# Query and key rows kept in DRAM as three slots of one stride, in a fused attention and feed-forward block

## The chip, the cores and the metric

The kernel runs on one core of a Trainium2 chip. Its time is device microseconds for one execution. The core has five engines that run side by side, each through its own list of instructions in order: TensorE (PE, matrix products), VectorE (DVE), ScalarE (ACT), GpSimd (POOL) and SyncE (SP, which here only issues transfers). Transfers (DMAs) are issued by SP and by ACT, and move data between DRAM and the on-chip memory (SBUF, 128 partitions) while the engines compute. Products land in PSUM banks, from which DVE and ACT copy them out.

## The reference

One transformer block over S = 2048 tokens of D = 640 features, all in f32: sliding-window attention with 32 heads of 20 features and a window of 256 keys, then a gated feed-forward layer of F = 1536.

```python
def _A_ref(x, wqkv, wo):                       # H = 32, Dh = 20, W = 256
    qkv = (x @ wqkv).reshape(B, S, 3, H, Dh).transpose(2, 0, 3, 1, 4)
    q, k, v = qkv[0], qkv[1], qkv[2]
    scores = jnp.einsum("bhqd,bhkd->bhqk", q, k) * (Dh ** -0.5)
    mask = (idx[:, None] - idx[None, :] >= 0) & (idx[:, None] - idx[None, :] < W)
    p = softmax(jnp.where(mask, scores, -1e9))
    o = jnp.einsum("bhqk,bhkd->bhqd", p, v)
    return o.transpose(0, 2, 1, 3).reshape(B, S, D) @ wo

h = x + _A_ref(layernorm(x), A_wqkv, A_wo)
h2 = h + (gelu(layernorm(h) @ w_gate) * (layernorm(h) @ w_up)) @ w_down
```

## The kernel before

**Numbers in two parts.** To keep f32 accuracy on f16 products, an operand is split into a high f16 part (`hi`) and a low one (`lo`, the rest), and a product of two operands is the sum of three: high with high, high with low, low with high.

**Tiling.** Tokens go in 16 blocks of 128 (`B[j]`) and 8 chunks of two blocks (`C[c]`, 256 tokens, `CW`). For each chunk, `qk(c, 0)` computes the queries and `qk(c, 1)` the keys, as features by tokens: five tiles of 128 features (`KC = 5`), two to a PSUM bank of the name `mm`, so three banks' worth (two tiles, two tiles, one tile). There are two such banks. The very first, `qk(0, 0)`, uses f32 products on the raw weights; the other 15 use three f16 products. `vproj(j)` computes the values of a block in two halves, in the same two banks.

**From product to stacked rows.** `qk_out` (line 750) empties a bank: ACT writes the high part into a tile `qks`, DVE writes the low part beside it, and the bank is free (`done("mm")`). Then ACT issues one transfer (line 764) that stores the tile to a DRAM buffer `qk<c><which>` of 640 feature rows, each with its high and its low 256 tokens. `qks` is a ring of two tiles, and line 754 lets ACT begin a tile only when fewer than two are begun and not yet stored. After the third store `stack(c, which, d)` (line 771) starts: from DRAM it loads, for each of the two heads of a pair (`par`), three sets of 20 rows into partitions 64 x par + 0..59 of `qT` (queries, one tile a chunk) or `kT` (keys, a ring of six blocks): high, high, low for queries and high, low, high for keys. One product over 60 rows then gives the three-part sum. So a chunk has 12 such loads, each of 20 partitions with 16 runs of 256 tokens (512 bytes), 160 KB, issued by SP. The host orders the features of the weights (line 1684) as (head of the pair, feature of the head, pair), so the first half of the 640 rows belongs to `par = 0`.

**Around it.** For each block, `maxima` (line 842) forms raw scores with 60-row products and DVE takes each row's largest after adding a mask (`max_out`, line 914; `mask` for the first two blocks, `band` after); the maxima go back as two more rows of `qT` (partitions 60, 61, against rows of `kT` that hold powers of two, set by `big_lane`), and `scores` (line 959) forms the scores again with 62-row products, already less the maximum. ACT takes the exponential into `pt`, POOL sets masked entries to zero, `value_lane` multiplies by the values, `normalise` divides (it copies `pv` through the tile `oT`), and `wo_block` projects. The feed-forward layer follows (the last scores are formed at 566 us) and shares no code with the change.

**What sets the order.** All instructions are put out by a program that runs ahead of time: a loop (line 1632) over lanes (generators) with a model of the chip, `Clock`. Each step names its engine and when its inputs will be ready by the model; `cost` (line 214) gives durations, `box` (line 74) says which bytes an access touches, `issue` (line 162) advances the model's time, with at most eight transfers in flight (`window`, line 69). The order on each engine comes out of this model; on the chip each engine runs through its list and waits where data is late. While no score has been formed and TensorE would be idle in the model, the loop puts out a product of `ident16` with itself into `pv` (line 1663), a placeholder without use for the result. `stack` waits in the model for the stores, for `pos["big"]`, and for the weights (chunks 0 and 1) or for block 2c-3 having been scored; for chunks from 2 on its loads are spread out by `PACE`.

Of the kernel before, what the change touches and what calls it, by code (L numbers as in the profile page):

```python
# [11 lines left out]
F32 = mybir.dt.float32  # L12
F16 = mybir.dt.float16
BF16 = mybir.dt.bfloat16
# [8 lines left out]
P = 128  # L23
# [30 lines left out]
class Clock:  # L54
# [18 lines left out]
    @staticmethod  # L73
    def box(ap):

        t = ap.tensor
        size = mybir.dt.size(ap.dtype)
        (ps, pn), *free = [tuple(x) for x in ap.ap]
        if ap.space == DRAM:
            n = 1 + sum((c - 1) * abs(st) for st, c in [(ps, pn), *free])  # L80
            return t.name, (0, 1, ap.offset * size, (ap.offset + n) * size, n * size, 1, 1)
        if ps:
            p0, f0 = divmod(ap.offset, ps)
        else:
            p0, f0 = 0, ap.offset
        n = 1 + sum((c - 1) * abs(st) for st, c in free)
        step, count = max(((abs(st), c) for st, c in free if c > 1), default=(n, 1))
        run = n - (count - 1) * step
        if run >= step:
            run, count = n, 1  # L90
        return t.name, (p0, p0 + pn, f0 * size, (f0 + n) * size, run * size, step * size, count)
# [98 lines left out]
class Engine:  # L190
# [23 lines left out]
    def cost(self, op, out, ins):  # L214
        n = out.free_size()
        if op.startswith("dma_start"):
            size = math.prod(c for _, c in out.ap) * mybir.dt.size(out.dtype)
            if op == "dma_start_transpose":
                return size / 150e3
            wide = mybir.dt.size(out.dtype) == 4 or out.space == DRAM  # L220
            return size / (380e3 if wide else 150e3)
        half = mybir.dt.size(out.dtype) == 2 and ins and mybir.dt.size(ins[0].dtype) == 2
        if self.name == "tensor":
            n = ins[1].free_size()
            if op == "transpose":
                n = ins[0].partition_size()
            passes = 1 if mybir.dt.size(ins[0].dtype) == 2 else 2 if op == "transpose" else 4
            rows, cols = ins[0].partition_size(), out.partition_size()
            mode = "full" if op == "transpose" else "row" if rows <= 64 else "col"
            mode = "full" if mode == "col" and cols > 32 else mode  # L230
            k = self.clock
            switch, k.mode = SWITCH * (k.mode != mode), mode
            at = out.start_partition() + (ins[0].start_partition() // 4 if mode == "row" else 0)
            beside, k.half = mode != "full" and at > k.half and not switch, at
            if beside:
                return 0.0005
            return switch + k.warmth(max(n * passes / 2400, 0.027), rows) + 0.0027
        if self.name == "vector":
            m = max([n] + [i.free_size() for i in ins])
            if op == "tensor_copy" and half or op == "tensor_scalar" and m > 320:  # L240
                return (0.065 if half else 0.185) + 0.00053 * m
            return 0.065 + 0.00106 * m + 0.06 * (op == "scalar_tensor_tensor" and len(ins) == 3)
        if self.name == "scalar":
            return 0.00084 * n + (0.05 if op == "copy" or len(ins) == 1 else
                                  0.14 if ins[0].space == PSUM else 0.18)
        if self.name == "gpsimd":
            if op == "memset":
                return 0.06 + 0.0008 * n
            return 0.46 if n == 1 else 0.06 + (0.00105 if op == "affine_select" else 0.00203) * n
        raise NotImplementedError(self.name)  # L250
# [3 lines left out]
def block_kernel(ctx: ExitStack, tc: tile.TileContext, x, wqkv, wo, wg, wu, wd, out):  # L254
# [67 lines left out]
    def on(eng, *reads, when=None, after=None):  # L322
        f = need(*reads, when=when, eng=eng)
        if after is not None:
            return (eng,), lambda: max(f(), nc.others(after, eng))
        return (eng,), f
# [14 lines left out]
    nc.vector.tensor_copy(ident16, ident)  # L341
    mhalf = const.tile([P, 1], F32, name="mhalf")
    nc.vector.memset(mhalf, -0.5)
    ones = const.tile([P, P], F32, name="ones")
    nc.vector.memset(ones, 1.0)


    NS = 16
# [229 lines left out]
    def ff_scales_down(fg):  # L578
# [19 lines left out]
    gu = gu.rearrange("p (a c f) -> p a c f", c=KC, f=512)  # L598

    HB = P // 2  # L600
    mask = wp.tile([P, 2 * P], F32, name="mask")
    nc.gpsimd.memset(mask, 0.0)
    nc.gpsimd.affine_select(mask[:, P:2 * P], mask[:, P:2 * P], pattern=[[-1, P]],
                            compare_op=ALU.is_ge, fill=NEG, base=0, channel_multiplier=1)
    band = wp.tile([P, 5 * HB], F32, name="band")
    nc.gpsimd.memset(band, 0.0)
    for a in range(2):
        first, last = band[HB * a:HB * a + HB, 0:HB], band[HB * a:HB * a + HB, 4 * HB:]
# [116 lines left out]
    def qk(c, which):  # L725
# [3 lines left out]
        if not first:  # L729
            xh, xl = C[c].x  # L730
            wh, wl = w.hl
        d = dram.tile([D, 2, CW], F16, name=f"qk{c}{which}")
        left = [3]
        for t0 in range(0, KC, 2):
            ts = range(t0, min(t0 + 2, KC))
# [14 lines left out]
    def qk_out(c, which, ts, ps, d, left):  # L750

        o = ps[:, :len(ts) * CW].rearrange("p (t n) -> p t n", n=CW)
        up = qs if c == which == 0 else _pow2(QE)
        yield on("scalar", ps, when=lambda: pos["qk"] < pos["qks"] + 2 and (c or pos["qs"]))
        pos["qk"] += 1
        st = nc.tile(wq, [P, 2, 2, CW], F16, "qks", 2)
        hi, lo = (st[:, :len(ts), i, :] for i in range(2))
        nc.scalar.activation(hi, o, AF.Copy, scale=up)
        yield on("vector", hi, after=ps)
        nc.vector.scalar_tensor_tensor(lo, o, up, hi, op0=ALU.mult, op1=ALU.subtract)  # L760
        done("mm")
        both = st[:, :len(ts)].rearrange("p t m n -> p t (m n)")
        yield on("scalar", both)
        nc.scalar.dma_start(d[ts[0] * P:(ts[-1] + 1) * P].rearrange("(t p) m n -> p t (m n)", p=P),
                            both)
        pos["qks"] += 1
        left[0] -= 1
        if not left[0]:
            side.append((LATE, stack(c, which, d)))

    def stack(c, which, d):
        yield ("sync",), need(d, when=lambda: pos["big"] == 2 and (W["q"].ready if c < 2 else
                                                                B[2 * c - 3].scored), eng="sync")
        if which == 0:
            C[c].qT = at("qT", [P, H // 2, CW], F16)
            for b in (2 * c, 2 * c + 1):
# [3 lines left out]
            s = 2 * c % RK  # L780
            to = kT[:, :, s:s + 2, :].rearrange("p i r n -> p i (r n)")
        for par in range(2):
            for m, i in enumerate(((0, 0, 1), (0, 1, 0))[which]):
                rows = slice(64 * par + DH * m, 64 * par + DH * m + DH)
                if c > 1:
                    yield ("sync",), lambda: nc.moved["sync"] - PACE
                nc.sync.dma_start(to[rows], d.rearrange("(a d i) m n -> a m d i n", a=2,
                                                        d=DH)[par, i])
        C[c].stacked += 1
        if C[c].stacked == 2:  # L790
            for b in (2 * c, 2 * c + 1):
# [886 lines left out]
def _layout(inputs):  # L1678
# [2 lines left out]
    f = lambda n: np.asarray(inputs[n])  # L1681
    c = np.ascontiguousarray
    wqkv = f("A_wqkv").reshape(KC, P, 3, D).transpose(2, 1, 0, 3).copy()
    order = np.arange(D).reshape(H // 2, 2, DH).transpose(1, 2, 0).reshape(-1)
    wqkv[:2] = wqkv[:2][..., order]
    rows = lambda a: a.reshape(KC, P, FG, F // FG).transpose(2, 1, 0, 3)
    return {
# [29 lines left out]
```

## Time and profile before

| | |
|---|---|
| median of three runs | 1014.78 us (1012.98 to 1014.88) |
| the profiled execution | 1015.33 us |
| its span, first to last instruction | 1013.6 us |
| busy PE / DVE / ACT / POOL | 996.3 / 754.7 / 442.5 / 315.0 us |
| mean granted TensorE clock | 0.997 of full |
| loads of query and key rows on SP's queue | 48 and 48, 160 KB each |
| stores of query and key tiles on ACT's queue | 32 of 256 KB and 16 of 128 KB |

A row of the grouped view reads: line, engine, operation, output <- inputs, shape, xcount | busy us, mean ns of one | idle time of the engine just before them and what ended it. Every instruction goes through one helper, so all have line L199, and one goes by names of tiles. A row of the order of time reads: start us, duration us, engine, line, operation, names, shape, count [idle before <- what ended it]. SPq and ACTq are the transfer issues of SP and ACT. A row of the windows gives the stretch, its length, busy time of PE, PEld (weight loads), DVE, ACT and POOL, the granted clock, the share of the DMA engines and GB/s. Matmul records overlap, since products are pipelined.

### The profile page before, as it was taken

How to read it: one execution, taken by the hardware profiler on the slowest of the kernel's cores; microseconds unless marked ns; L12 is line 12 of the kernel's file. 1: busy time of each engine (PE TensorE's matmuls, PEld its weight loads, DVE VectorE, ACT ScalarE, POOL GpSimd, SP SyncE). 2: the span in 40 equal slices, each digit the busy share in tenths (PEclk: the TensorE clock that was granted, in tenths of full speed). 3: DMA queues.
4: the chain of work that ended last, by engine and by line, in shares of the span. 5: the costliest groups of instructions: out<-in, count | busy, mean ns of one | idle time of the engine just before them, and what ended most of it. 6: DMA issues, size and time to landing. Idle time of an engine off the chain costs nothing.

```text
span 1013.6 us, 30516 instructions
## 1 busy us (share of the span) xinstructions
PE 996.3 (98%) x12798; PEld 696.4 (69%) x12798; DVE 754.7 (74%) x2212; ACT 442.5 (44%) x711; POOL 315.0 (31%) x504
## 2 busy tenths in 40 slices
PE   8999999999999999999999999999999999999998
PEld 7876777666666776776655654577777777777776
DVE  7888999786667877676688687798888875544553
ACT  5516666654555555554567634432222212221220
POOL 7004344643344333332345311254313300000000
PEclk9999999999999999999999999999999999999999
DMA  8658775291271714236004342323453542222211
GB/s 308 148 127 177 185 163 167 67 166 41 71 133 39 143 55 88 64 79 188 18 29 133 68 130 92 98 107 116 144 187 102 148 142 78 79 103 80 78 53 52
DMA packets 105834, 112.67 MB, mean 111 GB/s; under 512 B 38368, under 2 KB 79584, under 8 KB 105696
## 3 DMA queue, kind: packets, MB, share of 16 engines
q1 hardware_dynamic: 93600, 99.97, 36.7%
q10 hardware_dynamic: 12096, 10.75, 3.5%
q8 instruction: 100, 1.64, 0.7%
q14 instruction: 38, 0.31, 0.1%
HBM read 73.73 MB, written 28.84 MB: 101 GB/s over the span
## 4 chain that ended last, share of the span: by engine, by line
PE 86%; DVE 7%; DMA 3%; ACT 2%; issue 1%; SPq 1%; POOL 0%; ACTq 0%; DVEq 0%
PE mm L199 44%; PE pv L199 12%; PE ra L199 12%; PE rb L199 10%; PE tp L199 7%; DVE junk L199 1%; DMA kT<-qk 1%; SPq L199 1%; DVE am L199 1%; DMA wst<-in_wu_dram 1%; DMA qT<-in_wqkv_dram 1%; DMA wst<-in_wg_dram 1%; ACT pt L199 1%; DVE ht L199 0%; DVE w1l L199 0%
## 5 line engine op out<-in xcount | busy, mean ns | idle before, releaser
L199 POOL TENSOR_SCALAR_AFFINE_SELECT pt<-pt 128x512 f32<-128x512 f32 x352 | 174.8, 512 | 297.0 <-ACT pt L199 281.3
L199 DVE CUSTOM_DVE_ANT_0 junk<-rb,band 128x320 bf16<-128x320 f32 x228 | 111.5, 489 | 53.4 <-PE rb L199 48.8
L199 ACT ACTIVATE pt<-ra,esc 128x640 f32<-128x640 f32 (+2 forms) x132 | 100.6, 770 | 74.3 <-PE ra L199 69.3
L199 DVE CUSTOM_DVE_ANT_0 junk<-ra,band 128x320 bf16<-128x320 f32 x220 | 107.7, 489 | 33.2 <-PE ra L199 26.8
L199 ACT ACTIVATE pt<-rb,esc 128x640 f32<-128x640 f32 (+2 forms) x124 | 94.1, 764 | 82.4 <-PE rb L199 73.2
L199 PE MATMUL pv<-pt,v 128*21 128x128 f32 x2880 | 104.7, 279 | 0.0
L199 PEld LDWEIGHTS <-ah 128*128 128x128 f16 x768 | 75.1, 98 | 29.2 <-issue 1.9
L199 ACT ACTIVATE gel<-gel,ffk 128x512 f32<-128x512 f32 x36 | 26.0, 722 | 134.3 <-DVE gel L199 134.3
L199 PEld LDWEIGHTS pv<-pt,v 128*21 128x21 f32 x2880 | 70.0, 101 | 9.9 <-issue 1.0
L199 PEld LDWEIGHTS <-ws 128*128 128x128 f16 x720 | 70.5, 98 | 8.1
L199 PEld LDWEIGHTS <-qT 60*64 60x64 f16 x1280 | 29.8, 104 | 61.0 <-issue 51.9
L199 PEld LDWEIGHTS <-kT 62*64 62x64 f16 x2880 | 63.4, 107 | 11.2 <-issue 7.5
L199 PEld LDWEIGHTS <-gu 128*128 128x128 f16 x440 | 41.9, 98 | 36.1 <-issue 2.5
L199 DVE SCALAR_TENSOR_TENSOR ht<-mm,ffk,ht 128x320 f32<-128x320 f32 x96 | 52.1, 545 | 13.7 <-PE mm L199 11.8
L199 ACT CAST ah<-gel 128x512 f16<-128x512 f32 x48 | 29.6, 617 | 68.7 <-DVE gel L199 68.6
L199 PE MATMUL mm<-xh,w1h 128*128 128x256 f16 x200 | 54.6, 273 | 0.8 <-DVE qks L199 0.8
L199 PE MATMUL mm<-xl,w1h 128*128 128x256 f16 x200 | 54.7, 274 | 0.0
L199 PE MATMUL mm<-xh,w1l 128*128 128x256 f16 x200 | 54.6, 273 | 0.0
L199 POOL TENSOR_TENSOR gelt<-gelt 128x256 f32<-128x256 f32 x18 | 15.3, 852 | 112.0 <-ACT gelt L199 111.9
L199 PE MATMUL mm<-w3h,oh 128*128 128x320 f16 x160 | 48.3, 302 | 1.4 <-DVE qks L199 1.4
L199 PE MATMUL mm<-w3l,oh 128*128 128x320 f16 x160 | 48.2, 301 | 0.0
L199 PE MATMUL mm<-w3h,ol 128*128 128x320 f16 x160 | 48.1, 300 | 0.0
(313 smaller groups left out, 2562.6 us busy)
## 6 DMA issues: line engine op xcount, KB each, us to landing
ws<-wsums SPq DMA_DIRECT2D x24, 640.0 KB
qk<-qks ACTq DMA_DIRECT2D x32, 256.0 KB
qT<-qk SPq DMA_DIRECT2D x48, 160.0 KB
kT<-qk SPq DMA_DIRECT2D x48, 160.0 KB
wsums<-ws SPq DMA_DIRECT2D x12, 640.0 KB
ht<-in_x_dram SPq DMA_DIRECT2D x16, 320.0 KB
h_dram<-ht SPq DMA_DIRECT2D x16, 320.0 KB
ht<-h_dram SPq DMA_DIRECT2D x16, 320.0 KB
```

Of the source, the lines that this page charges most:

```text
L199: r = real(*args, **kw)
```

## The change

The DRAM buffer becomes three slots of 640 rows, `[3, D, CW]` instead of `[D, 2, CW]`: queries as high, high, low, keys as high, low, high. ACT writes the high part twice into a `qks` tile of three parts (one instruction over an input repeated by a stride of zero), DVE writes the low part as before. Each tile of 128 features is stored by a transfer of its own, five for a query or key half instead of three, of 192 KB each. The host's feature order becomes (feature of the head, head of the pair, pair), so the three slots and the 20 features of a head lie at one stride, and `stack` reads the 60 rows of a head of the pairs by one transfer: two loads for a query or key half instead of six, 480 KB each. In DRAM such a row is 16 runs of 512 bytes in one piece.

Beside this, the third key tile of chunk 0 uses the tile `oT`, not in use yet, in place of the `qks` ring (`spare`), and does not wait for the ring. The first query loads no longer wait for the whole split query weight but for the parts that lie in the tile they overwrite, and the first key loads do not wait for it at all. `mask` and `band` become bf16, the unused `ones` goes. In the model, DRAM accesses get boxes with strides, and the rate of 2-byte loads goes from 150e3 to 170e3 bytes per us.

```diff
@@ Clock.box
         if ap.space == DRAM:
-            n = 1 + sum((c - 1) * abs(st) for st, c in [(ps, pn), *free])
-            return t.name, (0, 1, ap.offset * size, (ap.offset + n) * size, n * size, 1, 1)
-        if ps:
+            p0, pn, f0, free = 0, 1, ap.offset, [(ps, pn), *free]
+        elif ps:
@@ Engine.cost
-            return size / (380e3 if wide else 150e3)
+            return size / (380e3 if wide else 170e3)
@@ constants
-    ones = const.tile([P, P], F32, name="ones")
-    nc.vector.memset(ones, 1.0)
-    mask = wp.tile([P, 2 * P], F32, name="mask")
+    mask = wp.tile([P, 2 * P], BF16, name="mask")
-    band = wp.tile([P, 5 * HB], F32, name="band")
+    band = wp.tile([P, 5 * HB], BF16, name="band")
@@ qk
-        d = dram.tile([D, 2, CW], F16, name=f"qk{c}{which}")
+        d = dram.tile([3, D, CW], F16, name=f"qk{c}{which}")
@@ qk_out
-        yield on("scalar", ps, when=lambda: pos["qk"] < pos["qks"] + 2 and (c or pos["qs"]))
+        spare = c == 0 and which == 1 and len(ts) == 1
+        yield on("scalar", ps, when=lambda: (spare or pos["qk"] < pos["qks"] + 2)
+                 and (c or pos["qs"]))
         pos["qk"] += 1
-        st = nc.tile(wq, [P, 2, 2, CW], F16, "qks", 2)
-        hi, lo = (st[:, :len(ts), i, :] for i in range(2))
-        nc.scalar.activation(hi, o, AF.Copy, scale=up)
+        if spare:
+            st = at("oT", [P, 4, P], F32, 1).bitcast(F16).rearrange("p a n -> p (a n)")
+            st = st[:, :3 * CW].rearrange("p (t m n) -> p t m n", t=1, n=CW)
+        else:
+            st = nc.tile(wq, [P, 2, 3, CW], F16, "qks", 2)
+        twice, lo = ((st[:, :len(ts), 0:2, :], st[:, :len(ts), 2, :]),
+                     (st[:, :len(ts), 0:3:2, :], st[:, :len(ts), 1, :]))[which]
+        hi = twice[:, :, 0]
+        nc.scalar.activation(twice, o.unsqueeze(2).to_broadcast([P, len(ts), 2, CW]), AF.Copy,
+                             scale=up)
...
-        both = st[:, :len(ts)].rearrange("p t m n -> p t (m n)")
-        yield on("scalar", both)
-        nc.scalar.dma_start(d[ts[0] * P:(ts[-1] + 1) * P].rearrange("(t p) m n -> p t (m n)", p=P),
-                            both)
+        for i, t in enumerate(ts):
+            yield on("scalar", st[:, i])
+            nc.scalar.dma_start(d[:, t * P:(t + 1) * P].rearrange("m p n -> p m n"), st[:, i])
@@ stack
-        yield ("sync",), need(d, when=lambda: pos["big"] == 2 and (W["q"].ready if c < 2 else
-                                                                B[2 * c - 3].scored), eng="sync")
+        def free():
+            if c > 1:
+                return B[2 * c - 3].scored
+            return pos["big"] == 2 and (which or len(W["q"].have) > (2, KC - 1)[c])
+
+        yield ("sync",), need(d, when=free, eng="sync")
...
         for par in range(2):
-            for m, i in enumerate(((0, 0, 1), (0, 1, 0))[which]):
-                rows = slice(64 * par + DH * m, 64 * par + DH * m + DH)
-                if c > 1:
-                    yield ("sync",), lambda: nc.moved["sync"] - PACE
-                nc.sync.dma_start(to[rows], d.rearrange("(a d i) m n -> a m d i n", a=2,
-                                                        d=DH)[par, i])
+            if c > 1:
+                yield ("sync",), lambda: nc.moved["sync"] - PACE
+            nc.sync.dma_start(to[64 * par:64 * par + 3 * DH],
+                              d.rearrange("m (d a i) n -> a (m d) i n", a=2, d=DH)[par])
@@ _layout
-    order = np.arange(D).reshape(H // 2, 2, DH).transpose(1, 2, 0).reshape(-1)
+    order = np.arange(D).reshape(H // 2, 2, DH).transpose(2, 1, 0).reshape(-1)
```

## The prediction

> **What bounds the kernel now.** I read the page first (span, busy times, chain that ended last), then TensorE's waits, then the order of time around each gap.
>
> ```profile
> span 1013.6 us, 30516 instructions
> ...
> PE 996.3 (98%) x12798; PEld 696.4 (69%) x12798; DVE 754.7 (74%) x2212; ACT 442.5 (44%) x711; POOL 315.0 (31%) x504
> ...
> PE 86%; DVE 7%; DMA 3%; ACT 2%; issue 1%; SPq 1%; POOL 0%; ACTq 0%; DVEq 0%
> ```
>
> TensorE is busy in 996.3 of 1013.6 us and carries 86% of the chain. The change takes no matrix product away, so it can only win what is not product: idle time (17.3 us), placeholder products, and time at a lower clock. The placeholders are the loop's `ident16` products, issued while no score exists:
>
> ```profile
> L199 PE MATMUL pv<-ident 128*128 128x128 f16 x221 | 16.5, 239 | 2.5 <-DVE pv L199 2.5
> ```
>
> Those before 26 us cover the loading of inputs, which the change leaves alone. The later runs, in TensorE's order of time (start, duration):
>
> ```profile
> 37.95 3.29 PE L199 MATMUL pv<-ident 128*128 128x128 f16 x56
> ...
> 41.08 0.76 PE L199 MATMUL mm<-gu 128*128 128x320 f32 x2
> ...
> 51.81 0.31 PE L199 MATMUL ra<-kT,qT 60*64 60x128 f16 x8
> ...
> 70.22 1.95 PE L199 MATMUL pv<-ident 128*128 128x128 f16 x32
> ```
>
> The first run is a hole of 41.08 - 37.95 = 3.1 us, 56 ns a placeholder. Two thirds of the rest up to the first score stand in the run at 70.22 (32 of 55 or so, together some 3.1 us). The row at 51.81 is the first product that reads stacked rows (the first maxima). Of the idle time, three waits touch what is changed. First the list of waits (us in total, times, longest), then the two rows of TensorE's order that waited for key rows:
>
> ```profile
> PE mm L199 <- DVE qks L199: 2.2, 3, 0.8
> ```
>
> ```profile
> 229.55 0.32 PE L199 MATMUL rb<-kT,qT 60*64 60x64 f16 x3 [2.14 <-DMA kT<-qk]
> ...
> 297.31 0.33 PE L199 MATMUL ra<-kT,qT 60*64 60x320 f16 x3 [1.37 <-DMA kT<-qk]
> ```
>
> The two waits for key rows are 3.5 us. They cost more than that, as the windows behind them show (each row ends with granted clock, DMA share and GB/s):
>
> ```profile
> 228.00:234.00 6.00, 4.45 (x59) 2.67 (x60) 2.04 (x9) 0.79 (x1) 0.00 (x0) 0.72 0.05 10
> 297.00:301.00 4.00, 3.69 (x79) 2.71 (x78) 1.00 (x4) 0.79 (x1) 1.42 (x3) 0.57 0.80 226
> ```
>
> The clock falls to 0.57 for 4 us after the second wait, 4 x 0.43 = 1.7 us lost; around the first, 6 x 0.28 = 1.7, of which I count 1.5, since TensorE idles in a part of it. So late key rows cost 3.5 + 3.2 = 6.7 us.
>
> **Why those rows come late.** The SP queue around both places, then the chain's pieces at the second, and one store of the ACT queue:
>
> ```profile
> 200.49 3.17 SPq L199 DMA_DIRECT2D qT<-qk  x4
> ...
> 221.29 1.38 SPq L199 DMA_DIRECT2D ht<-in_x_dram  x1
> 222.72 2.36 SPq L199 DMA_DIRECT2D kT<-qk  x3
> ...
> 272.21 4.72 SPq L199 DMA_DIRECT2D qT<-qk  x6
> ...
> 283.31 9.72 SPq L199 DMA_DIRECT2D kT<-qk  x5
> ```
>
> ```profile
> 286.98 3.72 DMA qk<-qks
> ...
> 290.71 0.74 SPq L199
> ...
> 292.29 4.99 DMA kT<-qk
> ```
>
> ```profile
> 221.78 0.34 ACTq L199 DMA_DIRECT2D qk<-qks  x1
> ```
>
> Counting the 48 stores in order (three per query or key half of a chunk), the one at 221.78 is the last of chunk 4's keys. Its rows were stored 60 us before the loads that begin at 283.31; yet the load at 290.71 waited for the store of 286.98, which belongs to chunk 5. That is no data dependence. The planner's `window` (line 69, eight transfers) models it: a transfer waits for an older one to finish. Chunk 3's keys likewise sat behind an input tile's load at 221.29. From its first issue to its last byte chunk 3 took 200.49 to 229.4 (just before the product that waited; 28.9 us) and chunk 4 272.21 to 292.29 + 4.99 = 297.28 (25.1 us), where chunk 6, undisturbed, ran through:
>
> ```profile
> 393.02 4.73 SPq L199 DMA_DIRECT2D qT<-qk  x6
> 397.79 6.99 SPq L199 DMA_DIRECT2D kT<-qk  x6
> ```
>
> ```profile
> 396.00:410.00 14.00, 14.00 (x278) 9.33 (x276) 9.33 (x37) 8.77 (x14) 5.54 (x12) 1.00 0.78 126
> ```
>
> Twelve loads of 160 KB at 126 GB/s (last figure) are 15.6 us, so the last lands some 17 us after the first issue.
>
> **The change part by part.**
>
> A. *The third key tile of chunk 0 no longer waits for the ring of two `qks` tiles* (`spare`, taken from the unused `oT`). Before, ACT and DVE copied it out at:
>
> ```profile
> 36.36 0.38 ACT L199 ACTIVATE qks<-mm 128x256 f16<-128x256 f32 x1 [2.04 <-DVE sw L199]
> ...
> 39.54 0.42 DVE L199 SCALAR_TENSOR_TENSOR qks<-mm,qks 128x256 f16<-128x256 f32 x1
> ```
>
> ACT idled 2.04 us before it, DVE had other work first, and the second half of the value projection needs that bank: hence the 3.1 us of placeholders. Copied out at once (0.38 and 0.42 us, a little more for the wider write) the bank is free before 37.95. I take **-3.1 us**; bounds 0 (DVE, busy there, puts it off again) and -6.2 (the other 55 placeholders go too).
>
> B. *Six loads of 20 rows become two of 60 rows.* SP issues 32 instead of 96; each waits for its turn in the eight and can be stood behind. TensorE wanted chunk 3's keys at 229.55 - 2.14 = 227.4, 26.9 us after the first issue, and chunk 4's at 297.31 - 1.37 = 295.9, 23.7 us after. Four issues that run through like chunk 6's twelve land after 17 us at the old rate: 7 to 10 us early. The rate itself is a cost the trace doesn't show. Bounds: unchanged (126 GB/s), since key rows still land in runs of 512 bytes; or the fastest window of wide rows here, since query rows are now 8 KB whole on both sides:
>
> ```profile
> 297.00:298.00 1.00, 0.69 (x22) 0.53 (x25) 0.32 (x1) 0.10 (x1) 0.00 (x0) 0.79 1.15 350
> ```
>
> At 350 GB/s a chunk's 1.97 MB would take 5.6 us, with the 2 us of lag seen above 7.6. I take the first end, 17 us, by which B already holds. Against it: rows now alternate between the halves within each feature tile, so both loads need all five stores, where the first three of six used to need only the first four tiles. Chunks 3 and 4 had their stores long before; chunks 0 to 2 feel it, where TensorE waits for no key row now. I take **-5.0 us**, three quarters of 6.7, since a new order can place a late load elsewhere; bounds -6.7 and +2 (nothing won, and one more wait like the first at chunks 0 to 2).
>
> The Trainium skill (DMA: Bandwidth & Descriptors, Why a DMA increments its semaphore by 16, "How many engines") says a transfer spreads over the largest number up to 16 that divides both patterns' slowest dimension: 10 engines for 20 rows, 15 for 60. By it a key load of 480 KB would take two thirds of its old time and B would stay the same, only safer; no row here shows the engines one by one.
> The skill (TensorE: Matmul & The Clock Gate, Part 1) halves the clock after a whole idle window of about 3.4 us. By that neither wait would cost clock and B would shrink to three quarters of 3.5, -2.6; the 0.57 row above says that a wait of 1.4 us did cost it, and the trace decides.
>
> C. *Stores and copies grow.* Rows before:
>
> ```profile
> L199 ACT ACTIVATE qks<-mm 128x512 f16<-128x512 f32 x30 | 17.9, 596 | 16.5 <-PE mm L199 12.8 <-DMA qT<-qk 2.0 <-PE rb L199 1.4
> ...
> L199 ACT ACTIVATE qks<-mm 128x256 f16<-128x256 f32 x15 | 5.8, 383 | 8.5 <-PE mm L199 3.9 <-DVE sw L199 2.0 <-DMA qk<-qks 1.3
> ```
>
> ```profile
> L199 ACTq DMA_DIRECT2D qk<-qks x48: 338/366/436, 19.5 to 461.8; - x48
> L199 SPq DMA_DIRECT2D qT<-qk x48: 739/742/948, 29.4 to 453.1; - x48
> ```
>
> The high part is written twice: (596 - 383)/256 = 0.83 ns an element, so +0.43 us on 32 copies and +0.21 on 16, 17 us of ACT. Stores go from 48 to 80: 32 more at 0.37 (as now) to 0.74 (as SP's loads of many short rows) is 12 to 24 us. ACT, busy 442.5 us, has room:
>
> ```profile
> 300.00:400.00 100.00, 99.91 (x1907) 68.84 (x1900) 74.50 (x273) 55.41 (x84) 38.49 (x80) 1.00 0.32 76
> ```
>
> 55 of 100 us becomes about 63. What shows is the `mm` bank held 0.43 us longer: TensorE waited for that in 3 of 48 tiles, so 3 x 0.43 = 1.3 us; bounds 0 and, were half exposed, 24 x 0.43 = 10. I take **+1.0**.
>
> D. *At nothing:* masks in bf16. DVE's row with a 16-bit second operand costs what the all-f32 one does (686 and 689 ns), so the 489 ns of the maxima stay; if not, DVE at 74% has cover.
>
> ```profile
> L199 DVE CUSTOM_DVE_ANT_0 junk<-rb,band 128x320 bf16<-128x320 f32 x228 | 111.5, 489 | 53.4 <-PE rb L199 48.8
> ...
> L199 DVE TENSOR_TENSOR ol<-tp,oh 128x512 f16<-128x512 f32 x16 | 11.0, 686 | 1.8 <-ACT oh L199 1.8
> ...
> L199 DVE TENSOR_TENSOR rs<-pv,rr 128x512 f32<-128x512 f32 x18 | 12.4, 689 | 37.6 <-PE pv L199 37.0 <-POOL rr L199 0.6
> ```
>
> `ones` is unused, the feature order is made on the host, the 170e3 and the DRAM boxes steer only the planner, and chunk 0's earlier query load is not the last piece there: its keys are.
>
> **Sum.** 1015.33 (profiled execution; its span is 1013.6, 1.7 us lie around it) - 3.1 - 5.0 + 1.0 = 1008.2. That execution is 0.55 above the median 1014.78, so the median forecast is 1007.7, said as **1008**. Its own range is 1003 (A and B at their ends, C nothing: 1014.8 - 6.2 - 6.7 = 1001.9, a little inside) to 1012.
>
> **Rivals.**
> 1. *The startup alone is won.* The planner remakes the whole order, and late rows turn up at other chunks, two waits with their clock as now: 1014.8 - 3.1 + 1.0 = 1012.7. For it: planned landings are never the real ones; against: 7 to 10 us of slack.
> 2. *Hidden anyway.* DVE is 86.92 of 100 us busy between 20 and 120, and TensorE waits for it at 93 us:
>
> ```profile
> 20.00:120.00 100.00, 98.29 (x1211) 73.69 (x1212) 86.92 (x310) 55.58 (x106) 23.44 (x33) 1.00 0.69 160
> ```
>
> ```profile
> 93.97 0.33 PE L199 MATMUL ra<-kT,qT 60*64 60x320 f16 x4 [0.88 <-DVE mxs L199]
> ```
>
> Products that start 3.1 us earlier would wait there as much longer, and B comes back as waits elsewhere: 1014.8 - 3.1 + 3.1 - 5.0 + 5.0 = 1014.8. Against: this 0.88 us is the longest wait for DVE that stands there.
> 3. *Slower: ACT stands behind its stores.* ACT already waits for unrelated transfers:
>
> ```profile
> ACT qks L199 <- DMA qT<-qk: 2.0, 1, 2.0
> ```
>
> With five stores a set instead of three, two of them beyond what the eight slots let pass, ACT can wait 2 us in each of 16 sets, and the exponentials behind it keep a score bank. If TensorE pays a quarter, 16 x 0.5 = +8, B is lost and A kept: 1014.8 - 3.1 + 8 = 1019.7. It decides once TensorE pays over 3.1/16 = 0.2 us a set. Against: ACT is free for some 45 of 100 us in the row of 300 to 400.
> 4. *All of it is won:* the other 55 placeholders, all of the key rows and the 2.2 us for `qks`: 1014.8 - 6.2 - 6.7 - 2.2 = 999.7. Against: C makes `qks` later, not earlier.
>
> **Numbers.** Forecast 0.49, rival 1 0.13, rival 2 0.13, rival 3 0.20, rival 4 0.05. A measurement tells 0.2%, 2 us. Rival 1 (2.1 us) straddles that bound; faster 0.49 + 0.05 + 0.12 = 0.66, within 0.13 + 0.01 = 0.14, slower 0.20. The range 1002 to 1018 holds the forecast and the first two rivals, and leaves out most of rivals 3 and 4.
>
> **What would show it.** Right: no placeholders between 37 and 42 us and first maxima (51.8 us now) some 3 to 5 us earlier; TensorE's list of waits without `kT<-qk`, clock 1.00 between 220 and 310; ACT near 475 us busy; junk rows still 489 ns. Wrong: new TensorE waits on `pt`, `mm` or `qks` of more than 5 us, ACT idle before `DMA qk<-qks`, or key loads slower than 17 us a chunk.

## The result: about 1% slower, and the profile after

The changed kernel takes 1023.98 us (median of 4 runs, 1020.89 to 1026.72), the kernel before 1013.88 us beside it (4 runs, 1011.36 to 1014.88). The ratio is 1.0103, with a 95% interval of 1.0066 to 1.0139. So the change makes this kernel slower by about 1%, where 1008 us was forecast and 1018 was the upper end of the range.

The page of the changed kernel: span, busy times, and the engines' shares of the chain that ended last.

```profile
span 1023.0 us, 30610 instructions
...
PE 1000.6 (98%) x12877; PEld 700.4 (68%) x12877; DVE 747.9 (73%) x2211; ACT 459.0 (45%) x711; POOL 314.1 (31%) x504
...
PE 84%; DVE 7%; DMA 3%; ACT 3%; issue 2%; POOL 1%; SPq 1%; ACTq 0%; DVEq 0%; POOLq 0%
```

Span is TensorE's busy time and its idle time. Busy went from 996.3 to 1000.6 us (+4.3), idle from 17.3 to 22.4 (+5.1); together they are the 9.4 us between the two spans. The busy part is placeholders. Their group, by line, after the change:

```profile
L198 PE MATMUL pv<-ident 128*128 128x128 f16 x300 | 21.4, 231 | 2.4 <-DVE pv L198 2.4
```

Before there were 221 of them in 16.5 us, so they add 4.9 us, and all other products are 0.6 us shorter. The idle time is best seen by stretches. First the kernel before, then the changed one (window, its length, TensorE's busy time; the last three figures are granted clock, DMA share and GB/s):

```profile
20.00:130.00 110.00, 108.29 (x1318) 80.07 (x1317) 95.82 (x351) 58.87 (x112) 24.60 (x35) 1.00 0.71 163
260.00:520.00 260.00, 257.51 (x5039) 177.57 (x5037) 186.61 (x683) 140.70 (x217) 98.49 (x205) 0.99 0.37 87
130.00:260.00 130.00, 126.05 (x2281) 90.58 (x2280) 105.78 (x381) 79.14 (x127) 58.34 (x105) 0.99 0.49 115
```

```profile
20.00:130.00 110.00, 105.52 (x1316) 77.60 (x1315) 92.36 (x337) 60.41 (x106) 24.38 (x29) 0.98 0.65 167
260.00:520.00 260.00, 254.12 (x4953) 178.66 (x4953) 174.91 (x651) 144.79 (x213) 96.43 (x202) 0.99 0.38 94
...
130.00:260.00 130.00, 127.99 (x2315) 91.69 (x2313) 108.90 (x399) 85.40 (x131) 57.95 (x106) 1.00 0.57 133
```

Idle in 20 to 130 us grew from 1.7 to 4.5 us, in 130 to 260 it fell from 4.0 to 2.0, in 260 to 520 it grew from 2.5 to 5.9. The list of TensorE's waits (us in total, times, longest) names the new ones:

```profile
PE ra L198 <- issue: 2.7, 2, 1.8
PE pv L198 <- issue: 2.6, 2, 1.5
PE pv L198 <- DVE pv L198: 2.4, 1, 2.4
PE rb L198 <- DVE mxs L198: 1.9, 2, 1.2
PE rb L198 <- ACT pt L198: 1.8, 3, 0.8
PE tp L198 <- DVE am L198: 1.7, 2, 1.5
```

No row of that list has a wait for stacked key rows any more, and the two stretches that had lost clock before now run at 1.00 without a gap:

```profile
228.00:234.00 6.00, 6.00 (x124) 4.43 (x116) 5.37 (x26) 3.58 (x6) 2.96 (x7) 1.00 0.17 63
297.00:301.00 4.00, 4.00 (x98) 3.26 (x96) 2.09 (x9) 1.59 (x2) 1.42 (x3) 1.00 0.36 115
```

What the loads were to win is there, then. Three losses stand against it: 4.9 us of placeholders, 5.3 us of waits named "issue" (four of them, at 287 to 415 us), and about 2.7 us of waits for VectorE at 95 to 102 us. The clock is not one of them. In either profile it falls to half speed for 3.41 us twice, from 229.31 and 297.57 us before and from 101.94 and 344.28 us after, so it loses 3.4 us in both, and its mean is 0.997 in both.

The placeholders come after the hole that the prediction looked at. TensorE's order of time after the change:

```profile
35.62 1.22 PE L198 MATMUL pv<-ident 128*128 128x128 f16 x19
...
42.34 1.11 PE L198 MATMUL pv<-ident 128*128 128x128 f16 x17
...
54.26 0.31 PE L198 MATMUL rb<-kT,qT 60*64 60x128 f16 x8
...
69.27 1.22 PE L198 MATMUL pv<-ident 128*128 128x128 f16 x19
...
70.94 1.74 PE L198 MATMUL pv<-ident 128*128 128x128 f16 x28
...
72.96 2.69 PE L198 MATMUL pv<-ident 128*128 128x128 f16 x45
```

The hole of 56 at 37.95 is now 19 and 17, but between 50 and 94 us there are 142 placeholders where there had been 55. The first maxima come at 54.26 us, 2.5 us later than before. The key loads of chunk 0, which they need, start later too, since SP holds them back for the landing of the spare tile's store. The waits of SP's queue, and its order of time:

```profile
SPq L198 <- DMA qk<-oT: 9.2, 1, 9.2
```

```profile
43.39 0.93 SPq L198 DMA_DIRECT2D kT<-qk  x2
```

The same loads before:

```profile
40.14 4.83 SPq L199 DMA_DIRECT2D kT<-qk  x6
```

That the late loads make the placeholders is not shown. TensorE does not wait at 54.26 us; where the maxima and the placeholders stand is the planner's choice. In e11 below, the same work with another constant, the key loads begin at 43.81 us and the first maxima at 53.78, and only 57 placeholders stand between 50 and 94 us.

### The profile page after: what moved, and what is told of

It is laid out like the page before. It is cut to its first block, busy times and chain, and to the rows that moved or that the text cites. A ratio compares the mean times of both kernels' runs of the same rounds, so it can differ in the third digit from the quotient of the medians.

```text
span 1023.0 us, 30610 instructions
## 1 busy us (share of the span) xinstructions
PE 1000.6 (98%) x12877; PEld 700.4 (68%) x12877; DVE 747.9 (73%) x2211; ACT 459.0 (45%) x711; POOL 314.1 (31%) x504
## 4 chain that ended last, share of the span: by engine, by line
PE 84%; DVE 7%; DMA 3%; ACT 3%; issue 2%; POOL 1%; SPq 1%; ACTq 0%; DVEq 0%; POOLq 0%
PE mm L198 43%; PE pv L198 12%; PE ra L198 12%; PE rb L198 10%; PE tp L198 7%; ACT pt L198 1%; DVE junk L198 1%; DMA qk<-qks 1%; DMA wsl<-h_dram 1%; POOL pt L198 1%; DMA qT<-mT 1%; SPq L198 1%; DVE am L198 1%; DMA wst<-in_wu_dram 0%; DVE ht L198 0%
## 5 line engine op out<-in xcount | busy, mean ns | idle before, releaser
L198 DVE CUSTOM_DVE_ANT_0 junk<-ra,band 128x320 bf16<-128x320 f32 x246 | 120.4, 490 | 50.9 <-PE ra L198 44.8
L198 ACT ACTIVATE pt<-rb,esc 128x640 f32<-128x640 f32 (+2 forms) x138 | 106.3, 775 | 82.2 <-PE rb L198 50.3
L198 DVE CUSTOM_DVE_ANT_0 junk<-rb,band 128x320 bf16<-128x320 f32 x202 | 98.9, 490 | 45.0 <-PE rb L198 40.1
L198 ACT ACTIVATE pt<-ra,esc 128x640 f32<-128x640 f32 (+2 forms) x118 | 88.2, 755 | 69.8 <-PE ra L198 50.1
L198 ACT ACTIVATE qks<-mm 128x1024 f16<-128x1024 f32 (+1 forms) x44 | 38.9, 884 | 25.2 <-DMA qk<-qks 8.9
L198 PE MATMUL mm<-xh,w0h 128*128 128x256 f16 x175 | 48.8, 279 | 0.0
L198 PE MATMUL mm<-xl,w0h 128*128 128x256 f16 x175 | 48.7, 279 | 0.0
```

Of the source, the lines that this page charges most:

```text
L198: r = real(*args, **kw)
```

## The experiments

Each ratio is to the kernel before on the same chip, with its 95% interval; it comes from the single runs and is not the quotient of the medians. The first theory was that one of the change's own parts costs the 10 us; its rivals were the other parts, and later the order that the planner writes.

### One part alone, one part undone (e1 to e4)

**e1: what "steers only the planner", the masks and `ones`, without slots, stores or loads.**

```
kernel before, plus
-            return size / (380e3 if wide else 150e3)
+            return size / (380e3 if wide else 170e3)
... the DRAM boxes of the change, mask and band in BF16, no ones
```

> The kernel before with only the planner's parts (170e3, boxes with strides for DRAM), the bf16 masks and without `ones`; two slots, three stores and six loads stay. Theory 'stores and loads' (the loss comes from the wider stores and the bunched loads): within 3 us of before, about 221 placeholders, no idle time of TensorE put down to 'issue'. Rival 'order' (any new order of the planner costs or wins some 10 us by luck): 5 us or more away from before, with its own placeholders and waits.

Measured 1012.77 against 1016.78 us, 0.9969 (0.9940 to 0.9998). No loss comes from these parts as such, with 207 placeholders and 16.6 us of idle time in the profile.

**e2: the six 20-row loads put back into the changed kernel.**

```
-                nc.sync.dma_start(to[64 * par:64 * par + 3 * DH], ...)
+            for m in range(3):
+                nc.sync.dma_start(to[64 * par + DH * m:...+ DH], ... [par, m])
```

> The changed kernel with its loads taken apart again: six of 20 rows for a query or key half (one slot each) in place of two of 60. Stores, copies and planner as changed. Theory 'bunched loads starve TensorE's own instructions' (5.3 us of idle time put down to 'issue' plus some 1.7 us of clock, all within 12 us after a chunk's loads): 'issue' goes to 0 on TensorE and the kernel is 5 to 7 us faster than the changed one, unless waits for key rows come back (6.7 us in the kernel before). Rival 'it is the stores': 'issue' may go, the placeholders stay near 300 and the time within 4 us of the changed kernel.

Measured 1031.14 us, 1.0135 (1.0078 to 1.0192). TensorE's waits for key rows are back, 5.2 us in three, where the changed kernel has none. The loads of 60 rows are not what loses. (These are not quite the loads of before: their rows lie in one piece in DRAM, and SP's median issue takes 0.32 and 0.40 us for queries and keys, where it took 0.74 before.)

**e3: two slots instead of three**, so a single write of the high part, stores of 128 KB, and per half a load of 20 rows and one of 40; the spare tile and the five stores stay.

```
-        d = dram.tile([3, D, CW], F16, name=f"qk{c}{which}")
+        d = dram.tile([2, D, CW], F16, name=f"qk{c}{which}")
...
-        nc.scalar.activation(twice, o.unsqueeze(2).to_broadcast(...), AF.Copy, scale=up)
+        nc.scalar.activation(hi, o, AF.Copy, scale=up)
```

> The changed kernel without the doubled high part: two slots in DRAM, ACT writes the high part once (0.6 us in place of 1.0), a store has 128 KB in place of 192, still five of them; loads of 20 and of 40 rows, four in place of two. Theory 'stores hold the ring' (ACT's waits for stores, 10.1 us, keep the product banks full at 50 to 76 us): ACT's waits for stores fall below 5 us, placeholders from 300 to 250 or fewer, 3 to 6 us faster than the changed kernel. Rival 'number of stores, not bytes': waits and placeholders stay.

Measured 1013.93 us, 0.9989 (0.9957 to 1.0022). The loss is gone, so I took the third slot for its cause.

**e4: the changed kernel without the spare tile.**

```
-        spare = c == 0 and which == 1 and len(ts) == 1
+        spare = False
```

> The changed kernel with chunk 0's third key tile back in the `qks` ring. By the prediction's part A (the tile out of the ring wins the 3.1 us hole at 38 us): 3 us slower than the changed kernel, with a run of 50 or so placeholders at 38 to 41 us. Rival: the hole's placeholders only move to 50 to 76 us, so the time stays within 2 us of the changed kernel.

Measured 1027.16 us, 1.0110 (1.0064 to 1.0155), not to be told from the changed kernel. 339 placeholders stand in the trace against 300, 39 x 56 ns = 2.2 us: the spare may win something like that, though this order was planned anew, and it doesn't make the loss.

### Copies or bytes (e5, e6)

**e5: e3 with the high part written twice, the second copy not stored.** **e6: the changed kernel with its three slots and 192 KB stores, but the loads of e3.**

```
e5:  e3, and st = nc.tile(wq, [P, 2, 3, CW], F16, "qks", 2), the double write of the change,
     then st = st[:, :, 1 - which:3 - which]
e6:  the changed kernel, and in stack() for each half
+            for m0, m1 in (((0, 1), (1, 3)), ((2, 3), (0, 2)))[which]:
+                nc.sync.dma_start(to[64 * par + DH * m0:64 * par + DH * m1], ...)
```

> Two slots, five stores of 128 KB and four loads as in e3, but ACT writes the high part twice again (1.0 us in place of 0.6; the second copy is not stored). Theory 'bytes of the stores' (what fills the ring is 192 KB a store, not ACT's longer copy): within 3 us of e3, 189 placeholders as built. Rival 'the longer copy holds the bank': back to within 3 us of the changed kernel.

> The changed kernel (three slots, 192 KB a store) with four loads of 20 and 40 rows as in e3 and e5; against e5 only the third slot's bytes are stored in addition. Theory 'bytes of the stores': 300 placeholders as built, 7 to 12 us slower than e5, within 4 us of the changed kernel. Rival 'the form of the loads': within 4 us of e5.

Measured 1027.36 us, 1.0136 (1.0103 to 1.0170), and 1028.06 us, 1.0154 (1.0121 to 1.0186). e5 stores no byte more than e3 and is 1.5% slower, so the bytes of the stores fall as the cause; e6 shows that e3 did not win by its loads. It looked as if the longer copy were it; e9 and e10 below disprove that.

### A third staging tile (e7, e8)

**e7: e3 with three `qks` tiles. e8: e1 with three.** In both, the ring of 2 in the condition and in the tile becomes 3.

> e3 with three `qks` tiles in the ring in place of two (two slots leave the room). Theory 'the ring waits for stores': ACT's waits for stores (13.1 us in e3) fall below 4 us, 143 placeholders as built in place of 180, 2 to 5 us faster than e3. Rival 'TensorE waits elsewhere then' (DVE, the maxima rows): same time as e3.

> The kernel before with the planner's parts and the bf16 masks (e1) and three `qks` tiles in the ring; its stores and loads as before. Theory 'the ring waits for stores': 126 placeholders as built in place of 207, 4.5 us fewer of them, 4 to 8 us faster than before. Rival: idle time grows by as much, same as e1 (3 to 4 us faster than before).

e7: 1014.42 us, 0.9999 (0.9976 to 1.0023), with the 143 placeholders but no time won over e3: its theory falls. e8: 1019.70 us, 1.0072 (1.0034 to 1.0109), with 126 placeholders, the fewest of all kernels here, and 1% slower than e1. Its profile has 25.9 us of idle time, 6.7 of it one wait for key rows, where e1 has 1.5. More room and fewer placeholders, and yet slower: this spoke for the order as the cause.

### The copy or the order (e9, e10)

All kernels so far were planned anew, so each part came with another order of everything. These two keep the order and change only the copy, or the reverse. In the traces 12745 of the 12757 products of e3 stand in e9 in the same order, and 12756 of the 12766 of e5 in e10; e3 and e5 have 6698 in common.

```
e9:  e5, but the planner is told the cost of a single write
         if self.name == "scalar":
+            n //= 1 + (op == "activation" and out.tensor.name.startswith("qks"))
e10: e3, but the planner is told the cost of a double write
         if self.name == "scalar":
+            n *= 1 + (op == "activation" and out.tensor.name.startswith("qks"))
```

> The two-slot kernel with the double write, as in e5, but the planner is told the cost of a single write, so that the order on TensorE is that of e3 (1423 of some 19500 rows of it stand otherwise). Theory COPY (the 0.43 us more that each of 48 tiles holds its bank and ScalarE is the loss of e5): 1.010 to 1.014 of before, as e5. Theory ORDER (the planner, told of longer copies, wrote another order with worse waits): 0.997 to 1.002, as e3.

> The two-slot kernel with the single write of e3, but the planner is told that each copy writes twice as much, so that the order on all engines is that of e5, row for row. COPY: the 17 us of ScalarE are gone and with them the loss, 0.998 to 1.003. ORDER: 1.010 to 1.016, as e5, with the idle time and the clock loss at the same places.

| | order of e3 | order of e5 |
|---|---|---|
| single write | e3: 0.9989 (0.9957 to 1.0022) | e10: 1.0119 (1.0070 to 1.0169) |
| double write | e9: 1.0015 (0.9989 to 1.0040) | e5: 1.0136 (1.0103 to 1.0170) |

The order is worth 1.2 to 1.3% in either row; the write 0.2 to 0.3% in either column, within the intervals. The traces of e5 and e10 say the same more sharply. First the busy times of e5 and three rows of its TensorE's order of time, then the same of e10:

```profile
PE 1001.3 (97%) x12766; PEld 696.0 (68%) x12766; DVE 751.8 (73%) x2211; ACT 458.2 (45%) x711; POOL 315.7 (31%) x504
```

```profile
97.08 0.62 PE L198 MATMUL tp<-ident,oT 117*128 117x117 f32 x4 [1.00 <-ACT oT L198]
...
101.27 0.64 PE L198 MATMUL ra<-qT,kT 62*64 62x128 f16 x16 [0.91 <-DVE am L198]
...
107.66 0.33 PE L198 MATMUL rb<-kT,qT 60*64 60x320 f16 x4 [1.02 <-ACT pt L198]
```

```profile
PE 1000.5 (98%) x12766; PEld 695.7 (68%) x12766; DVE 751.0 (73%) x2211; ACT 443.9 (43%) x711; POOL 316.4 (31%) x504
```

```profile
94.00 0.62 PE L198 MATMUL tp<-ident,oT 117*128 117x117 f32 x4 [1.00 <-ACT oT L198]
...
98.19 0.64 PE L198 MATMUL ra<-qT,kT 62*64 62x128 f16 x16 [0.89 <-DVE am L198]
...
104.59 0.33 PE L198 MATMUL rb<-kT,qT 60*64 60x320 f16 x4 [1.06 <-ACT pt L198]
```

ScalarE is 458.2 us busy in one and 443.9 in the other, and in this stretch (94 to 111 us in e5) TensorE waits at the same instructions, for the same releasers, as long to within 0.04 us, only 3.1 us earlier. In both the clock falls, to 0.76 and 0.73 on average between 90 and 115 us. These waits are written into the order. Not all are: those named "issue" fall at other places, at 485.64 us in e5 and at 283.79 and 484.57 in e10.

### Both kernels in other orders (e11 to e16, e18)

If the order is worth 1%, then the kernel before has good and bad orders too. Here only the planner's constant for 16-bit loads is changed, in the kernel before (150e3 there) and in the changed one (170e3); the work on the chip is the same but for the order and the placeholders.

```
-            return size / (380e3 if wide else 150e3)
+            return size / (380e3 if wide else 152e3)
```

> The changed kernel with one planner constant at 180e3 for 170e3; the chip's work is the same but for the order and for 86 fewer placeholder products (86 x 56 ns = 4.8 us). COPY and the placeholders alone: 1.0103 - 0.0047 = 1.0056, within 0.002. ORDER: anywhere from 0.995 to 1.020, and the idle time and clock loss of the profile move by several us against the changed kernel.

> The kernel before with one planner constant at 152e3 for 150e3; same work, same number of products but one, another order. If an order is worth nothing by itself: 0.998 to 1.002. ORDER: it can differ by 0.5 to 1% either way, by idle time and clock.

> The kernel before with the planner constant at 160e3 for 150e3. The chip's work is the same but for the order and for 27 placeholders fewer (27 x 56 ns = 1.5 us). If an order moves the time by up to 1% either way, as between 150e3 and 152e3 (0.9949): anywhere from 0.990 to 1.010. If the step to 0.9949 was an exception: 0.997 to 1.001.

> The kernel before with the planner constant at 170e3, the value that the changed kernel has; 15 placeholders fewer (0.8 us). Compared with the changed kernel at the same constant (1.0103) it gives one pair of orders in which only the rest of the change differs. Theory NEUTRAL (the work of the change costs at most 0.3%, the order made the rest): the pairs at 160e3, 170e3 and 180e3 differ by both signs or by less than 0.5% in the mean. Theory CHANGE (the three slots cost about 1% in any order): each pair differs by 0.5 to 1.5%.

> The kernel before with the planner constant at 180e3; 35 placeholders fewer (2.0 us). Its pair is the changed kernel at 180e3 (1.0026). NEUTRAL: 0.995 to 1.006. CHANGE: 0.988 to 0.998.

> The changed kernel with the planner constant at 160e3; 39 placeholders fewer than the changed kernel (2.2 us), 67 more than its pair, the kernel before at 160e3 (3.8 us, which the longer wait for the first maxima would make). NEUTRAL: 0.997 to 1.010, within 0.5% of its pair. CHANGE: 1.006 to 1.015, 0.5 to 1.5% above its pair.

> The changed kernel with the planner constant at 190e3, 87 placeholders fewer than at 170e3 (4.9 us): a fourth order of the same work. If the orders of the changed kernel scatter as those of the kernel before (0.9949 to 1.0193): 0.994 to 1.012, no wait for key rows, issue of 0 to 5 us. If the changed kernel is slow in itself: 1.005 to 1.015.

| constant | kernel before | changed kernel |
|---|---|---|
| 150e3 | 1 | |
| 152e3 | e12: 0.9949 (0.9925 to 0.9974) | |
| 160e3 | e13: 1.0062 (1.0043 to 1.0081) | e16: 1.0021 (0.9998 to 1.0045) |
| 170e3 | e14: 1.0193 (1.0148 to 1.0239) | 1.0103 (1.0066 to 1.0139) |
| 180e3 | e15: 1.0078 (1.0047 to 1.0108) | e11: 1.0026 (0.9995 to 1.0056) |
| 190e3 | | e18: 1.0075 (1.0049 to 1.0101) |

One number that only the planner reads moves the kernel before over 2.4%, from 1010.39 us to 1034.72, and the changed kernel over 0.8%. The theory that the change costs 1% in any order falls: in the three rows with both kernels the changed one is the faster, by 0.4, 0.9 and 0.5%. NEUTRAL, as it was put for e14, is missed as well, since the three have one sign and a mean of 0.6%; e15 lies outside both ranges that were set for it, and e18 inside both. Nor is the changed kernel shown to be the better one: equal constants are not equal orders (e1 has 170e3 too, and 0.9969), and the means of the two columns are both 1.0056, with a standard deviation of 0.9% over five orders and 0.4% over four. The difference of the two means has a standard error of about half a per cent, so whether the change is worth something on average is open to about one per cent either way. e12 beats both kernels, by nothing but another order.

What the orders of the kernel before lose is in part what the change removes. TensorE's waits and one window of e14, the slowest:

```profile
PE ra L199 <- DMA kT<-qk: 12.4, 3, 7.1
PE rb L199 <- DMA kT<-qk: 3.2, 1, 3.2
```

```profile
306.35 0.47 PE L199 MATMUL ra<-kT,qT 60*64 60x320 f16 x3 [7.13 <-DMA kT<-qk]
```

```profile
300.00:310.00 10.00, 3.65 (x29) 2.03 (x28) 1.35 (x5) 0.79 (x1) 0.00 (x0) 0.56 0.33 80
```

In total, TensorE waits for key rows (us) 3.5, 0, 2.3, 15.6 and 4.4 in the five orders of the kernel before, 1.5 in e1, 6.7 in e8 and 5.2 in e2, all with six loads of 20 rows; 0.5 to 1.4 in the six kernels with loads of 20 and 40 (e3, e5, e6, e7, e9, e10); and nothing in the changed kernel, e4, e11, e16, e17 and e18, all with 60-row loads. These are the waits that the lists name so. Two more products that read these rows waited, 1.8 us in e12 and 4.5 us in e2, and the lists put that down to a store (`qk<-qks`); the nothing of e12 is therefore uncertain.

### The waits named "issue" (e17)

The changed kernel has 5.3 us of them, in the middle of groups, 7 to 12 us after the issue of wide loads. The SP queue, TensorE's order, and two windows of the changed kernel:

```profile
332.46 0.80 SPq L198 DMA_DIRECT2D qT<-qk  x2
333.37 0.94 SPq L198 DMA_DIRECT2D kT<-qk  x2
```

```profile
341.18 0.30 PE L198 MATMUL ra<-qT,kT 62*64 62x128 f16 x9
343.30 0.22 PE L198 MATMUL ra<-qT,kT 62*64 62x64 f16 x3 [1.82 <-issue]
```

```profile
339.00:342.00 3.00, 2.48 (x60) 1.62 (x57) 2.11 (x9) 1.66 (x3) 1.29 (x3) 1.00 1.15 194
344.00:348.00 4.00, 4.00 (x53) 2.60 (x52) 1.00 (x4) 1.57 (x3) 0.28 (x1) 0.57 0.80 67
```

No semaphore and no transfer of the kernel is named as releaser, the DMA engines are full (1.15), and 1.7 us of clock follow (4 x 0.43). The page lists a DMA queue of the kind "instruction" (packets, MB, share of 16 engines):

```profile
q8 instruction: 100, 1.64, 0.7%
```

I supposed that it brings in TensorE's instructions, that these stand behind the loads, and doubled each load.

```
+            for again in range(2 if c > 1 else 1):
+                if c > 1:
+                    yield ("sync",), lambda: nc.moved["sync"] - PACE
+                nc.sync.dma_start(to[64 * par:64 * par + 3 * DH], ...)
```

> The changed kernel with each 60-row load of the chunks after 1 issued twice, the second over the same rows, so the bytes of a bunch double. Theory FETCH (the waits of TensorE named issue come from its own instructions, which are fetched by DMA and stand behind the bunched loads): issue grows from 5.3 us to 8 us or more, at places 5 to 15 us after a bunch, and the time to 1.013 or more. Rival CHANCE (they belong to this order, or to something else than the bytes): issue stays at or below 5.3 us, and what time is lost goes to waits for key rows.

Measured 1063.45 us, 1.0468 (1.0435 to 1.0501), and "issue" 2.6 us, half of what it was: the theory FETCH falls as it was put. Its rival is only half right, since no wait for key rows came. But the edit doubles the bytes without making a bunch denser. Each second copy is spaced by `PACE` as well, and the four loads that the changed kernel issues from 332.46 to 334.31 us are eight here, from 333.94 to 369.03. TensorE's busy time is 19.5 us longer for the same number of products, at a mean clock of 0.985 for 0.997. The profile shows 42.0 us of idle time, mostly waits for a weight tile and for engines:

```profile
PE tp L198 <- DVE ws L198: 6.7, 1, 6.7
PE rb L198 <- ACT pt L198: 5.1, 11, 1.1
PE ra L198 <- DVE mxs L198: 4.1, 7, 0.8
```

This order, too, was planned anew, so the 40 us are not the price of the bytes alone.

The traces say what e17 could not. The 20 profiles have 30 waits named "issue" by TensorE, of 0.19 to 3.33 us. Every one ends 2.5 to 3.1 us after a packet of queue q8, 16384 bytes, has started, where such packets mostly come 5 to 9 us apart between 120 and 565 us; in the changed kernel they start at 284.15, 291.39, 340.37 and 411.77, and TensorE goes on at 287.03, 294.32, 343.30 and 414.57. The queue has 100 such packets for 25754 products and weight loads of TensorE, some 257 for each, and neighbouring waits lie 256 of these apart (the first two of the changed kernel, the last two of e17) or twice that (the two of e6). By these counts TensorE stood waiting for the next part of its own instruction list. What delays the packet is less sure. In the 3 us before it the DMA share was 0.66 to 1.21, against a median of 0.33 before the other packets in that stretch, which fits full DMA engines; no run changed the density of the loads alone. "Issue" is 0 to 1.6 us in all seven kernels with the work of before (e1 and e8 with them) and 0.6 to 5.3 us in the thirteen others.

## Why the prediction was wrong

**The step that failed** is the frame of the sum. It took the profile of before, removed two holes, added a cost, and left every other wait and placeholder where it stood. The half sentence that let it do so is in D: "the 170e3 and the DRAM boxes steer only the planner", costed at nothing; the changed copies, stores and loads were likewise priced on the chip alone, though the planner reads their costs too. What steers the planner writes a new order for all engines, and every wait was up for a new draw. With the same work on the chip, an order is worth 1.2 to 1.3% between e3 and e5 (e9, e10); the constant alone costs the kernel before 1.9% (e14) or wins 0.5% (e12); and the changed kernel itself goes from 1.0103 to 1.0021 and 1.0026 by another constant (e16, e11). It is no fixed price: e1 has 170e3, the boxes and the masks of D, and 0.9969. The order drawn here has 79 placeholders more and 5.1 us more idle time than the profile of before. Which of the costs that the planner reads led to it is not shown, and that it fell on the slow side is, as far as these runs tell, bad luck.

**A (-3.1 us).** The bank is copied out earlier (VectorE begins at 36.74 us, before at 39.54), and the hole at 37.95 shrank from 56 to 36 placeholders in two places, so the mechanism is there in part. Without the spare there are 39 placeholders more, in an order of its own (e4). But the gain did not arrive: the placeholders behind grew from 55 to 142. The key loads of chunk 0 came 3.3 us later, since they need the store of that very tile; the prediction had named this, as the bound of +2 in B, and did not price it at the start. By e11 these late loads are not what makes the placeholders; the order is.

**B (-5.0 us).** Right, and more so than I gave it: 3.5 us of waits and 3.4 us of clock (3.2 in the sum) are gone from these places, and in no order of the changed kernel does TensorE wait for key rows. Only its size was a property of one order: the same six loads cost 0 to 15.6 us of waits in five orders of the kernel before. And the clock that was won here was lost again at other waits.

On the clock, the rule of the Trainium skill (TensorE: Matmul & The Clock Gate, Part 1), by which it halves after a whole idle window of about 3.4 us, is against the rows here once more: 0.57 over 4 us after a wait of 1.82 us. The Trainium skill's rule on how many engines share a transfer (DMA: Bandwidth & Descriptors, "How many engines") is not shown by any row.

**C (+1.0 us).** The copies grew as worked out: 1020 ns a tile of two against 596, that is 0.42 us. The cost, 0.26% and 0.17% in the two pairs of the two-slot kernel (2.6 and 1.7 us), cannot be told from 1.0 or from nothing. ACT is 459.0 us busy and not 475, because issuing stores is not counted as busy; I had added the stores to a figure that leaves them out.

**D, masks.** Right: the maxima take 490 ns with a band in bf16, 489 before. The groups by line of the changed kernel, the maxima and the copies of C:

```profile
L198 DVE CUSTOM_DVE_ANT_0 junk<-rb,band 128x320 bf16<-128x320 f32 x202 | 98.9, 490 | 45.0 <-PE rb L198 40.1
...
L198 ACT ACTIVATE qks<-mm 128x1024 f16<-128x1024 f32 x30 | 30.6, 1020 | 13.5 <-PE mm L198 6.5 <-DVE mxs L198 3.6 <-DVE xp L198 2.3
```

**The rivals.** The slower one, ScalarE behind its stores, had the right sign for a reason that does not hold. ScalarE's waits for stores did grow, from 1.3 us to 10.1, but e1 has 6.2 and e3 13.1 of them at ratios of 0.997 and 0.999, and TensorE's wait for `qks` fell from 2.2 to 0.3 us. Rival 1 said what happened, "the planner remakes the whole order", but let it only cancel B; the new order could cost more than the part that it cancels. Rival 2 saw the place: products wait for VectorE's maxima at 95 to 102 us.

**The signs.** Most of what was to show the prediction right came true: no wait for key rows, the clock at 1.00 from 220 to 310 us, the maxima at 490 ns. The earlier first maxima and ScalarE's 475 us did not. Of the signs of being wrong, ScalarE's waits for stores came (10.1 us). No sign looked at the placeholders behind 50 us or at waits that the profile of before does not have, and there the time went.

## What to carry to other kernels

Where a program computes the order of the work from a cost model, a change to any cost, size or constant replaces the whole order, and that alone can be worth more than the change: here 2.4% between two orders of the same work. Size this scatter first, with a constant that only the planner reads, and judge a change by the same order with and without the work (tell the planner the one cost and give the chip the other) or by several orders of each. Price a step of the change by what its wait costs over several orders, not by the one that the profile happens to show.

## What the runs showed that I had not expected

TensorE stops for up to 1.82 us in the changed kernel, and 3.33 us in e6, in the middle of a group with nothing named that it waits for. By the packets of the instruction queue it waits for its own instruction list; that the loads' bytes hold these packets up fits the traces and is not shown. One program on one chip scatters by more than the medians suggest: e3 ran between 1010.14 and 1021.77 us, so its profile (1019.72) shows waits that most of its runs may not have.
